# Where the first four attention states are made, and where the loads of chunks 4 to 9 stand in SyncE's queue

## The chip, the cores and the metric

One core of a Trainium2 chip runs the whole program: linear attention (RWKV style), then an MLP with squared ReLU, then an MLP with a soft-max gated activation and a layer norm. The metric is the device time of one execution in microseconds (us); lower is better. Instructions stand in a fixed order on each of TensorE (PE), VectorE (DVE), ScalarE (ACT), GpSimd (POOL) and SyncE (SP, which here issues every DMA); each of the five works through its own list in order and waits on semaphores for the others.

## What is computed

```python
# attention: B=4, H=8, S=768, D=48; one 48x48 state per batch and head
for t in range(S):
    kt, vt, rt = k[:, :, t], v[:, :, t], r[:, :, t]
    y[:, :, t] = einsum(rt, state + u*kt (x) vt)
    state = w * state + kt (x) vt
x = relu(y_as_tokens @ w_in)          # 3072 x 384 @ 384 x 2048
x = (x * x) @ w_out                   # @ 2048 x 384
h = x @ w2_in                         # @ 384 x 1024
solu = h * softmax(h)
out = (layernorm(solu) * g_ln) @ w2_out   # @ 1024 x 384
```

## The kernel before

The 3072 tokens are 24 chunks of 128 (chunk c is batch c % 4, piece c // 4 of the sequence). The attention of a chunk is a masked 128x128 score matrix per head plus the product with the state that the earlier pieces of its batch left. Chunks 0 to 3 are the first of their batch and need no state; for them a state must only be *made* for chunks 4 to 7. Chunks 4 and up run in half-chunks of 64 tokens.

The MLP works on blocks of 512 tokens (4 chunks). Its weights come as 64-bit floats: a weight *unit* (128x512 of `w_in`, 512 KB, or 128x384 of `w_out`, 384 KB) is loaded into one of six staging tiles `stg`, DVE turns it into 32-bit floats in three instructions (L610, L613, L616), ACT casts the high part (`wih` or `woh`, L628), POOL subtracts to get the low part (`wil` or `wol`, L629). `w1_conv` does that for one unit and then issues the load of the unit six places on, which must wait until POOL has freed the staging tile. There are 28 units: four groups of three `w_in` units and four `w_out` units.

The MLP's loop runs over *steps*: `p1` multiplies a block by 128 columns of `w_in` (nine matmuls on high and low parts: `wih,xh`, `wih,xl`, `wil,xh`), ACT and DVE make the squared ReLU and split it into `gh` and `gl`, `p2` multiplies by `w_out`. The first block has 20 steps: eight on 256 tokens, then twelve on 512. `p1` runs two steps ahead of `p2`.

What else has to happen in these 20 steps is hung on them by the table `side` (step to list of functions), in this order in the program: weight units (`w1_conv`); the states of chunks 0 to 3 (`first_state`, at steps 0 to 3: `prep_kt` scales k on DVE into `ktg`, L375; `pe_u` multiplies, L451; `dve_first` scales the product into the state `sg`, L491); and for chunks 4 to 7 the attention itself: `prep_rk` scales k and r (`kd`, L351, and the two halves of `mv`, L356, all on POOL), `prep_b` makes the diagonal (L385, L386 on POOL, L397 on DVE, L402 on POOL), `pe_u` (L464) and `pe_scores` (L437) run on PE, `dve_state` (L501, L502) and `dve_mask` (L481) on DVE, `pe_av_sub` (L541) on PE, and `split_x` hands the result to the MLP. `load_chunk` issues a chunk's loads: `kd` (224 KB, L241), `tok` (384 KB, L242), two `mv` (96 KB each, L244) and two `vs` (96 KB each, L246). Chunks 8 and up come in later steps (table `ev`).

The side table is not the final order. The framework's scheduler plays the program against its own estimate of times and writes each engine's list; what a function issues can stand well away from the step that it hangs on. A function's instructions keep their data dependences, and a few carry an explicit order (`add_manual_dep`, without a semaphore). So the lists of the built program are read beside the diff below.

Of the kernel before, what the change touches and what calls it, by code (L numbers as in the profile page):

```python
# [177 lines left out]
def rwkv_moe_moe2_kernel(ctx, tc, rkd, tok, tk2, wd, w, u, w_in, w_out, w2_in, w2_out, g_ln, out):  # L178
    nc = tc.nc
# [45 lines left out]
    def load_chunk(c, slots=None):  # L225
        if c >= NC:
            return
        i = (c % B) * CPB + c // B
        if c < B:
            if slots:  # L230
                rk_t[c] = wp.tile([GR, 2, NP, C], F32, tag=slots[0], name="rkw")
                tok_t[c] = wp.tile([C, 3, DM], F32, tag=slots[1], name="tokw")
            else:
                rk_t[c] = mv[c][:GR]
                tok_t[c] = ap.tile([C, 3, DM], F32, tag="tok", name="tok")
            nc.sync.dma_start(out=rk_t[c], in_=rkd[i])
            nc.sync.dma_start(out=tok_t[c], in_=tok[i])
            return
        rk_t[c] = ap.tile([GR, NP, C], F32, tag="kd", name="kd")
        tok_t[c] = ap.tile([128, 3, DM], F32, tag="tok", name="tok2")[:, :2]  # L240
        nc.sync.dma_start(out=rk_t[c], in_=rkd[i, :, 1])  # L241
        nc.sync.dma_start(out=tok_t[c], in_=tk2[i, :, :2])  # L242
        for j in range(2):
            nc.sync.dma_start(out=mv[c % 2][RO[j]:RO[j] + D, j], in_=rkd[i, RO[j]:RO[j] + D, 0])  # L244
            q = slice(CH * j, CH * (j + 1))
            nc.sync.dma_start(  # L246
                out=vs[c % 2][q, j].rearrange("q s p d -> q (s p d)"), in_=tk2[i, q, 2]
            )
# [117 lines left out]
    def prep_kt(c):  # L366
        if c < B:
            k, t = tok_t[c][:, 1], kpt
            i0, i1 = (a.rearrange("q (a j d) -> q a j d", a=NP, j=2) for a in (k, t))
            o = ktg[c % 2].rearrange("q (a j d) -> q a j d", a=NP, j=2)  # L370
        else:
            i0 = tok_t[c][:, 1].rearrange("q (s e) -> q s e", s=2)
            i1 = kp2.rearrange("q p d -> q (p d)").unsqueeze(1).to_broadcast([128, 2, NP * D])
            o = ktg[c % 2].rearrange("q (s e) -> q s e", s=2)
        nc.vector.tensor_tensor(out=o, in0=i0, in1=i1, op=ALU.mult)  # L375
# [33 lines left out]
    def pin(ins):  # L409

        tc.keep_in_program_order(ins)
# [33 lines left out]
    def pe_u(c, ub=1):  # L445
        kt = ktg[c % 2]
        if c < B:
            for p in range(NP):
                for j in range(2):
                    h = 2 * p + j  # L450
                    nc.tensor.matmul(  # L451
                        ps[RO[j]:RO[j] + D, ub, p * D:(p + 1) * D],
                        kt[:, h * D:(h + 1) * D],
                        tok_t[c][:, 2, h * D:(h + 1) * D],
                        start=(p == 0),
                        stop=(p == NP - 1),
                    )
            return
        for s in range(1 if c // B == CPB - 1 else 2):
            for p in range(NP):  # L460
                for j in range(2):
                    q = slice(CH * j, CH * (j + 1))
                    o = (s * NP + p) * D
                    pin(nc.tensor.matmul(  # L464
                        ps[RO[j]:RO[j] + D, ub, o:o + D], kt[q, o:o + D], vs[c % 2][q, j, s, p],
                        start=True, stop=True,
                    ))
# [19 lines left out]
    def dve_first(c, ub):  # L487

        for j in range(2):
            q = slice(RO[j], RO[j] + D)  # L490
            nc.vector.tensor_tensor(  # L491
                out=sg[c][q], in0=ps[q, ub, :NP * D].rearrange("p (a e) -> p a e", a=NP),
                in1=wm[q, 1].to_broadcast([D, NP, D]), op=ALU.mult,
            )
# [33 lines left out]
    def pe_av_sub(c, yb):  # L528

        rk_t.pop(c)  # L530
        tok_t.pop(c)
        y = ps[:, yb, :DM].rearrange("p (k i) -> p k i", k=KD)
        for s in range(2):
            i = slice(s * CH, (s + 1) * CH)
            for piece in (True, False):
                for k in range(KD):
                    p = KD if piece else k
                    for j in range(2):
                        v = vs[c % 2][:KR[j], j, s].rearrange("q p d -> q (p d)")
                        m, o = (64, p * D + 16 * k - D) if piece else (D, p * D)  # L540
                        pin(nc.tensor.matmul(  # L541
                            y[64 * j:64 * j + m, k, i], v[:, o:o + m], mv[c % 2][:KR[j], j, p, i],
                            start=True, stop=True,
                        ))
        xr_t[c] = y
# [47 lines left out]
    def load_unit(src, kind, g, eng):  # L593


        n = DM if kind else 512
        st = mp.tile([128, 512], src.dtype, tag="stg", bufs=NST, name="stg")[:, :n]
        if kind:
            eng.dma_start(out=st, in_=src[g * 128:(g + 1) * 128])
        else:  # L600
            eng.dma_start(out=st, in_=src[g[0] * 128:(g[0] + 1) * 128, g[1] * 512:(g[1] + 1) * 512])
        return st
# [32 lines left out]
        W1 += [(0, (k, g)) for k in range(KD)] + [(1, 4 * g + q) for q in range(4)]  # L635
    w_ld, w_st = [0], []

    def w1_load(n=1):
        for _ in range(n):
            if w_ld[0] < len(W1):  # L640
                kind, g = W1[w_ld[0]]
                w_st.append((kind, g, load_unit((w_in, w_out)[kind], kind, g, nc.sync)))
                w_ld[0] += 1

    def w1_conv():
        kind, g, st = w_st.pop(0)
        weight_tiles(kind, g // 4 if kind else g[1])
        if kind:
            split(st, woh[g // 4][:, g % 4], wol[g // 4][:, g % 4])()
        else:  # L650
            split(st, wih[g[1]][:, g[0]], wil[g[1]][:, g[0]])()
        w1_load()
# [239 lines left out]

    def first_state(c):
        prep_kt(c)
        pe_u(c, 0)
        dve_first(c, 0)
        del tok_t[c]


# [1 line left out]
    side = {i: [] for i in range(first_full)}  # L901
    first_m = {m: i for i, (n, m, c0, sz) in reversed(list(enumerate(steps))) if n == 0}
    for g in range(4):
        for q, n in enumerate((2, 2, 3) if g < 3 else (1, 1, 1, 1)):
            side[first_m[4 * g + q]] += [w1_conv] * n
    for c in range(4):
        side[c].append(lambda c=c: (first_state(c), load_chunk(4 + c) if c < 2 else None))
    for q, c in enumerate(range(4, 8)):
        t = 5 + 3 * q + (q > 0)
        side[t].append(lambda c=c: (prep_rk(c), put_state(c, 0), prep_kt(c), prep_b(c)))  # L910
        side[t + 1].append(lambda c=c: (pe_u(c), pe_scores(c), dve_state(c), dve_mask(c)))
        side[t + 2].append(lambda c=c: (pe_av_sub(c, 0), load_chunk(c + 2)))
        side[t + 3].append(lambda c=c: split_x(c))
    p1_at = [0]

# [18 lines left out]
    for q, t in enumerate(visits):  # L934
        c = 2 * B + q
# [11 lines left out]
    for i in range(first_full, nsteps):  # L947
        n, m, c0, sz = steps[i]
# [111 lines left out]
```

## Time and profile before

| | |
|---|---|
| median of 3 runs | 730.61 us (727.38 to 731.11) |
| the profiled execution | 729.26 us, span 727.6 us |
| PE busy in the span | 701.8 us (96%), 25.8 us without a matmul |
| DVE, ACT, POOL busy | 407.1 us (56%), 319.5 us (44%), 265.9 us (37%) |
| mean granted TensorE clock | 0.996 of full speed |
| chain that ended last | 85% of the span on PE, DMA, DVE, POOL 1% each |

The profiled execution lies 1.35 us below the median and inside the range of the three runs. Busy times are summed over the whole program; the shares of one stretch can be quite other, and the table of windows further down gives them by stage. A row of a timeline reads: start, duration, engine, line, operation, output<-input, shape, count, and in brackets the idle time before it with what ended it. A row with x2 is two instructions in one stretch. On SP the duration is that of issuing.

### The profile page before, as it was taken

How to read it: one execution, taken by the hardware profiler on the slowest of the kernel's cores; microseconds unless marked ns; L12 is line 12 of the kernel's file. 1: busy time of each engine (PE TensorE's matmuls, PEld its weight loads, DVE VectorE, ACT ScalarE, POOL GpSimd, SP SyncE). 2: the span in 40 equal slices, each digit the busy share in tenths (PEclk: the TensorE clock that was granted, in tenths of full speed). 3: DMA queues.
4: the chain of work that ended last, by engine and by line, in shares of the span. 5: the costliest groups of instructions: out<-in, count | busy, mean ns of one | idle time of the engine just before them, and what ended most of it. 6: DMA issues, size and time to landing. Idle time of an engine off the chain costs nothing.

```text
span 727.6 us, 13207 instructions
## 1 busy us (share of the span) xinstructions
PE 701.8 (96%) x5152; PEld 600.6 (83%) x5152; DVE 407.1 (56%) x752; ACT 319.5 (44%) x621; POOL 265.9 (37%) x297
## 2 busy tenths in 40 slices
PE   4789989999999999999999999999999999999996
PEld 3678868888888888888888888888899999999996
DVE  7899884444443334333322266515868777677771
ACT  1444645545455545544554455634333233322241
POOL 6969787254523333333221023802303030300000
PEclk9999999999999999999999999999999999999999
DMA  8956631222322212322160016221112000000001
GB/s 284 290 191 196 199 111 57 78 84 74 115 81 87 58 49 62 110 64 67 46 198 25 12 41 212 79 87 44 57 64 66 22 23 23 12 22 23 23 34 37
DMA packets 33832, 61.93 MB, mean 85 GB/s; under 512 B 7265, under 2 KB 16098, under 8 KB 33762
## 3 DMA queue, kind: packets, MB, share of 16 engines
q1 hardware_dynamic: 33762, 61.01, 26.7%
q8 instruction: 42, 0.69, 0.4%
q14 instruction: 28, 0.23, 0.1%
HBM read 48.41 MB, written 9.44 MB: 80 GB/s over the span
## 4 chain that ended last, share of the span: by engine, by line
PE 85%; DMA 1%; DVE 1%; POOL 1%; issue 1%; ACT 0%; SPq 0%; POOLq 0%; ACTq 0%
PE ps L670 8%; PE ps L692 8%; PE ps L689 8%; PE ps L688 8%; PE ps L672 8%; PE ps L671 8%; PE ps L838 5%; PE ps L837 5%; PE ps L840 5%; PE ps L774 5%; PE ps L776 5%; PE ps L775 5%; PE ps L821 3%; PE ps L514 2%; PE ps L437 2%; PE ps L464 2%
## 5 line engine op out<-in xcount | busy, mean ns | idle before, releaser
L678 DVE TENSOR_TENSOR gl<-ps,gh 128x512 fp32r<-128x512 f32 (+1 forms) x100 | 66.6, 667 | 178.7 <-ACT gh L677 177.4
L670 PE MATMUL ps<-xh,wih 128*128 128x512 f32 (+1 forms) x300 | 117.5, 393 | 1.7 <-DVE gl L678 1.1
L672 PE MATMUL ps<-xh,wil 128*128 128x512 f32 (+1 forms) x300 | 115.2, 385 | 2.3 <-POOL wil L629 2.3
L688 PE MATMUL ps<-gh,woh 128*128 128x512 f32 (+1 forms) x300 | 113.2, 383 | 1.9 <-ACT gh L677 1.9
L671 PE MATMUL ps<-xl,wih 128*128 128x512 f32 (+1 forms) x300 | 114.7, 383 | 0.1
L689 PE MATMUL ps<-gh,wol 128*128 128x512 f32 (+1 forms) x300 | 113.3, 384 | 0.0
L675 ACT ACTIVATE ps<-ps 128x512 f32<-128x512 f32 (+1 forms) x100 | 56.3, 564 | 129.3 <-PE ps L672 128.8
L356 POOL TENSOR_TENSOR mv<-mv,pt 48x512 f32<-48x512 f32 x40 | 51.4, 1286 | 87.5 <-DMA mv<-in_rkd_dram 87.0
L692 PE MATMUL ps<-gl,woh 128*128 128x512 f32 (+1 forms) x300 | 83.2, 382 | 0.0
L672 PEld LDWEIGHTS ps<-xh,wil 128*128 128x128 f32 x300 | 56.7, 189 | 14.4 <-POOL wil L629 3.4
L670 PEld LDWEIGHTS ps<-xh,wih 128*128 128x128 f32 x300 | 56.6, 189 | 13.9 <-DVE gl L678 1.5
L688 PEld LDWEIGHTS ps<-gh,woh 128*128 128x128 f32 x300 | 55.9, 188 | 13.0 <-ACT gh L677 2.1
L837 PE MATMUL ps<-w2oh,lth 128*128 128x384 f32 x192 | 65.2, 339 | 0.2 <-ACT lth L830 0.2
L671 PEld LDWEIGHTS ps<-xl,wih 128*128 128x128 f32 x300 | 56.8, 190 | 10.3 <-DVE xl L590 0.3
L838 PE MATMUL ps<-w2ol,lth 128*128 128x384 f32 x192 | 65.2, 340 | 0.0
L689 PEld LDWEIGHTS ps<-gh,wol 128*128 128x128 f32 x300 | 56.1, 189 | 11.0 <-issue 0.2
L692 PEld LDWEIGHTS ps<-gl,woh 128*128 128x128 f32 x300 | 55.7, 189 | 10.9
L677 ACT CAST gh<-ps 128x512 fp32r<-128x512 f32 (+1 forms) x100 | 56.9, 570 | 2.8
L676 ACT ACTIVATE ps<-ps 128x512 f32<-128x512 f32 (+1 forms) x100 | 56.4, 566 | 2.8
L774 PE MATMUL ps<-w2ih,xh 128*128 128x512 f32 x144 | 57.4, 399 | 0.0
L775 PE MATMUL ps<-w2il,xh 128*128 128x512 f32 x144 | 56.9, 395 | 0.0
L776 PE MATMUL ps<-w2ih,xl 128*128 128x512 f32 x144 | 56.8, 395 | 0.0
(122 smaller groups left out, 1174.9 us busy)
## 6 DMA issues: line engine op xcount, KB each, us to landing
stg<-in_w_in_dram SPq DMA_DIRECT2D x18, 512.0 KB, 6.2
stg<-in_w_out_dram SPq DMA_DIRECT2D x24, 384.0 KB, 4.1
tok<-in_tk_dram SPq DMA_DIRECT2D x20, 384.0 KB, 3.8
x2d<-stg SPq DMA_DIRECT2D x18, 256.0 KB, 2.5
x2r<-x2d SPq DMA_DIRECT2D x6, 768.0 KB, 4.9
out_dram<-ob SPq DMA_DIRECT2D x24, 192.0 KB, 1.9
kd<-in_rkd_dram SPq DMA_DIRECT2D x20, 224.0 KB, 3.9
mv<-in_rkd_dram SPq DMA_DIRECT2D x40, 96.0 KB, 2.4
```

What stands on the lines that cost most here:

```text
L670: nc.tensor.matmul(hp, wih[g][:, k, f], xh[:, k, cs], start=(k == 0), stop=False)
L671: nc.tensor.matmul(hp, wih[g][:, k, f], xl[:, k, cs], start=False, stop=False)
L672: nc.tensor.matmul(hp, wil[g][:, k, f], xh[:, k, cs], start=False, stop=(k == KD - 1))
L678: nc.vector.tensor_tensor(out=gl, in0=hp, in1=gh.bitcast(F32), op=ALU.subtract)
L688: nc.tensor.matmul(acc[e], woh[m // 4][:, m % 4, f], gh, start=start, stop=False)
L689: nc.tensor.matmul(acc[e], wol[m // 4][:, m % 4, f], gh, start=False, stop=False)
L692: nc.tensor.matmul(acc[e], woh[m // 4][:, m % 4, f], gl, start=False, stop=stop)
L774: nc.tensor.matmul(o, x2h[j][:, k, s], w2["ih"][:, k, fs], start=(k == 0), stop=False)
L775: nc.tensor.matmul(o, x2h[j][:, k, s], w2["il"][:, k, fs], start=False, stop=False)
L776: nc.tensor.matmul(o, x2l[j][:, k, s], w2["ih"][:, k, fs], start=False, stop=(k == KD - 1))
L837: nc.tensor.matmul(o, hi[:, m], w2["oh"][:, m], start=(m == 0), stop=False)
L838: nc.tensor.matmul(o, hi[:, m], w2["ol"][m // 4][:, m % 4], start=False, stop=False)
```

## The change

Three things change in the side table. The states of chunks 0 to 3 are made at steps 2, 5, 8 and 11 in place of 0, 1, 2 and 3, and their products go to PSUM bank 1, the one that later chunks use for theirs, in place of bank 0. The loads of chunks 4 to 9 hang on steps 2, 5, 8, 12, 14 and 17; before, chunks 4 and 5 were loaded right behind the states of chunks 0 and 1, and chunks 6 to 9 behind `pe_av_sub` of chunks 4 to 7. Each of these loads gets an order: on SP it may not stand ahead of the last weight load that the program had issued by then. And `pe_av_sub` is put ahead of the other functions of its step.

```diff
+    w_last = [None]
+    def behind_weights(load, *args):
+        n = len(nc.cur_bb.bb.instructions)
+        load(*args)
+        for i in nc.cur_bb.bb.instructions[n:]:
+            if i.engine == nc.sync.engine:
+                tc.add_manual_dep(
+                    i, w_last[0].name,
+                    mybir.DependencyInfo(mybir.DependencyClass.NoSync, mybir.DependencyReason.DATA),
+                    reason="behind_weights",
+                )
...
                 w_ld[0] += 1
+                w_last[0] = nc.cur_bb.bb.instructions[-1]
...
     def first_state(c):
         prep_kt(c)
-        pe_u(c, 0)
-        dve_first(c, 0)
+        pe_u(c)
+        dve_first(c, 1)
         del tok_t[c]
...
-    for c in range(4):
-        side[c].append(lambda c=c: (first_state(c), load_chunk(4 + c) if c < 2 else None))
+    for c, t in enumerate((2, 5, 8, 11)):
+        side[t].append(lambda c=c: first_state(c))
+    for c, t in zip(range(4, 10), (2, 5, 8, 12, 14, 17)):
+        side[t].append(lambda c=c: behind_weights(load_chunk, c))
...
-        side[t + 2].append(lambda c=c: (pe_av_sub(c, 0), load_chunk(c + 2)))
+        side[t + 2].insert(0, lambda c=c: pe_av_sub(c, 0))
```

The built lists differ from the first loads of chunk 4 to PE's 415th row of some 2610, that is inside the first block and the start of the second; behind that they are the same on every engine. Three places follow. Lines of the changed program are 15 to 17 higher from L640 on.

SP's list, first before: the loads of chunks 4 and 5 (all but `tok`) stand ahead of the seventh weight unit, `stg_189`, and its successors.

```order
L267 DMA ub2_85<-in_u_dram 64x4x48 x2
L241 DMA kd_361<-in_rkd_dram 112x512
L244 DMA mv0_95<-in_rkd_dram 48x512
L246 DMA vs0_97<-in_tk2_dram 64x384
...
L241 DMA kd_448<-in_rkd_dram 112x512
L246 DMA vs1_98<-in_tk2_dram 64x384
L244 DMA mv1_96<-in_rkd_dram 48x512
L599 DMA stg_189<-in_w_out_dram 128x384
```

SP's list now. `stg_189` to `stg_449` follow `ub2` directly; `stg_463` is the sixteenth weight unit, whose staging tile POOL frees with the low part of unit `stg_341`.

```order
L599 DMA stg_449<-in_w_out_dram 128x384
L601 DMA stg_456<-in_w_in_dram 128x512
L601 DMA stg_463<-in_w_in_dram 128x512
L241 DMA kd_476<-in_rkd_dram 112x512
L242 DMA tok2_477<-in_tk2_dram 128x768
L244 DMA mv0_95<-in_rkd_dram 48x512
L246 DMA vs0_97<-in_tk2_dram 64x384
L244 DMA mv0_95<-in_rkd_dram 48x512
L246 DMA vs0_97<-in_tk2_dram 64x384
L241 DMA kd_567<-in_rkd_dram 112x512
L242 DMA tok2_568<-in_tk2_dram 128x768
```

All six loads of chunk 4 moved from ahead of ten weight units to behind them. The next weight unit comes only after those of chunk 5.

POOL's list, before: the scaling of chunks 4 and 5 stands among and ahead of the low parts of units `stg_189` to `stg_341`.

```order
L351 TENSOR_TENSOR kd_361<-kd_361,pt_80 112x512
L629 TENSOR_TENSOR wol_335<-stg_133,woh_334 128x384
L356 TENSOR_TENSOR mv0_95<-mv0_95,pt_80 48x512 x2
L351 TENSOR_TENSOR kd_448<-kd_448,pt_80 112x512
L356 TENSOR_TENSOR mv1_96<-mv1_96,pt_80 48x512 x2
L629 TENSOR_TENSOR wol_335<-stg_189,woh_334 128x384
L629 TENSOR_TENSOR wil_481<-stg_212,wih_480 128x512
L629 TENSOR_TENSOR wil_481<-stg_243,wih_480 128x512
L629 TENSOR_TENSOR wil_481<-stg_341,wih_480 128x512
```

POOL's list now, the same place and on to the end of chunk 4's scaling.

```order
L629 TENSOR_TENSOR wol_335<-stg_133,woh_334 128x384
L629 TENSOR_TENSOR wol_335<-stg_189,woh_334 128x384
L629 TENSOR_TENSOR wil_443<-stg_212,wih_442 128x512
L629 TENSOR_TENSOR wil_443<-stg_243,wih_442 128x512
L629 TENSOR_TENSOR wil_443<-stg_341,wih_442 128x512
L629 TENSOR_TENSOR wol_724<-stg_348,woh_723 128x384
L351 TENSOR_TENSOR kd_476<-kd_476,pt_80 112x512
L385 TENSOR_TENSOR tok2_477<-tok2_477,ub2_85 128x384
L629 TENSOR_TENSOR wol_724<-stg_409,woh_723 128x384
L356 TENSOR_TENSOR mv0_95<-mv0_95,pt_80 48x512 x2
```

Six instructions (one `kd` and two `mv` for each of chunks 4 and 5) went behind four weight units and more.

PE's list, before: chunk 4's scores (L437) stand behind a whole `p1` and a `p2`.

```order
L464 MATMUL ps_63<-vs0_97,ktg0_89 48x48 x16
L670 MATMUL ps_63<-xh_203,wih_480 128x512
...
L692 MATMUL ps_63<-gl_619,woh_334 128x256 x3
...
L689 MATMUL ps_63<-gh_682,wol_754 128x512
L437 MATMUL ps_63<-mv0_95,kd_361 64x64 x16
```

PE's list now: the first scores stand after two matmuls of that `p1`.

```order
L707 MATMUL ps_63<-gl_542,woh_334 128x256 x3
L464 MATMUL ps_63<-vs0_97,ktg0_89 48x48 x16
L685 MATMUL ps_63<-xh_203,wih_442 128x512
L686 MATMUL ps_63<-xl_204,wih_442 128x512
L437 MATMUL ps_63<-mv0_95,kd_476 64x64
L687 MATMUL ps_63<-xh_203,wil_443 128x512
```

One row of scores (x1) moved forward past a `p2` and most of a `p1`; the other fifteen stand behind the `p2` that follows.

## Rows read from the trace of the kernel before

**Rows 1.** Windows: busy time (instructions) of each engine by stretch, clock, DMA share, GB/s.

```profile
24.00:33.00 9.00, 6.05 (x35) 5.59 (x34) 6.35 (x14) 4.04 (x12) 9.00 (x9) 0.81 0.87 218
...
45.00:60.00 15.00, 13.89 (x174) 12.57 (x174) 14.68 (x31) 9.33 (x23) 9.68 (x10) 1.00 0.68 223
60.00:88.00 28.00, 27.97 (x294) 22.77 (x291) 26.93 (x53) 16.26 (x33) 23.94 (x24) 1.00 0.65 196
88.00:105.00 17.00, 14.78 (x160) 11.42 (x159) 12.99 (x23) 6.44 (x12) 13.26 (x13) 1.00 0.50 153
105.00:165.00 60.00, 60.00 (x582) 49.72 (x581) 29.02 (x56) 31.50 (x64) 31.46 (x31) 1.00 0.23 70
```

**Rows 2.** Timeline of PE, 28 to 104 us: rows that stood idle first.

```profile
28.70 0.76 PE L688 MATMUL ps<-gh,woh 128*128 128x256 f32 x3 [1.88 <-ACT gh L677]
...
49.80 0.39 PE L670 MATMUL ps<-xh,wih 128*128 128x256 f32 x1 [1.11 <-DVE gl L678]
...
97.95 0.51 PE L672 MATMUL ps<-xh,wil 128*128 128x512 f32 x1 [0.18 <-POOL wil L629]
...
100.61 1.59 PE L541 MATMUL ps<-mv,vs 112*64 112x64 f32 x48 [0.99 <-DVE mv L481]
...
103.92 0.50 PE L672 MATMUL ps<-xh,wil 128*128 128x512 f32 x1 [1.06 <-POOL wil L629]
```

**Rows 3.** Timeline of DVE, 44 to 93 us.

```profile
44.98 2.62 DVE L375 TENSOR_TENSOR ktg<-tok,kpt 128x384 f32<-128x384 f32 x2
...
49.32 0.42 DVE L678 TENSOR_TENSOR gl<-ps,gh 128x256 fp32r<-128x256 f32 x1
...
92.76 0.55 DVE L397 TENSOR_REDUCE b<-tok 128x8 f32<-128x384 f32 x1 [3.82 <-POOL mv L402]
```

**Rows 4.** Timeline of POOL, 33 to 90 us.

```profile
33.17 1.29 POOL L351 TENSOR_TENSOR kd<-kd,pt 112x512 f32<-112x512 f32 x1
...
39.47 2.60 POOL L356 TENSOR_TENSOR mv<-mv,pt 48x512 f32<-48x512 f32 x2
...
45.82 1.35 POOL L629 TENSOR_TENSOR wil<-stg,wih 128x512 fp32r<-128x512 f32 x1 [0.24 <-ACT wih L628]
...
54.51 1.02 POOL L386 TENSOR_TENSOR tok<-tok 128x384 f32<-128x384 f32 x1
...
58.75 1.37 POOL L402 TENSOR_SCALAR_AFFINE_SELECT mv<-b 64x512 f32<-64x512 f32 x2
...
79.75 2.64 POOL L356 TENSOR_TENSOR mv<-mv,pt 48x512 f32<-48x512 f32 x2 [2.52 <-DMA mv<-in_rkd_dram]
...
89.14 1.28 POOL L351 TENSOR_TENSOR kd<-kd,pt 112x512 f32<-112x512 f32 x1 [1.73 <-DMA kd<-in_rkd_dram]
```

**Rows 5.** Source view of L375: duration in ns min/median/max of twenty.

```profile
L375 DVE TENSOR_TENSOR ktg<-tok,kp x20: 542/671/2347, 56.1 to 361.5; 128x384 f32<-128x384 f32 x20
```

**Rows 6.** Timeline of SP, 48 to 84 us.

```profile
48.25 0.38 SPq L601 DMA_DIRECT2D stg<-in_w_in_dram  x1
...
74.92 0.42 SPq L244 DMA_DIRECT2D mv<-in_rkd_dram  x1
...
83.83 0.39 SPq L241 DMA_DIRECT2D kd<-in_rkd_dram  x1
```

**Rows 7.** The page's DMA issues: count, KB each, median us from issue to landing.

```profile
kd<-in_rkd_dram SPq DMA_DIRECT2D x20, 224.0 KB, 3.9
```

**Rows 8.** Timeline of PE, 54 to 61 us.

```profile
54.27 0.56 PE L451 MATMUL ps<-tokw,ktg 128*48 128x48 f32 x16
...
55.58 0.40 PE L670 MATMUL ps<-xh,wih 128*128 128x512 f32 x1
...
57.65 0.52 PE L692 MATMUL ps<-gl,woh 128*128 128x256 f32 x3
...
59.30 0.92 PE L464 MATMUL ps<-vs,ktg 64*48 64x48 f32 x32
60.16 0.50 PE L670 MATMUL ps<-xh,wih 128*128 128x512 f32 x1
```

## The prediction

> **What bounds the kernel now.** I read the windows by stage first, since the page's 96% for PE is an average. From 105 us on PE is busy without a break for 60 us [rows 1], and it stays so up to the last part of the program, which the change does not touch. PE's idle time that the change can reach lies where its lists differ: between some 45 and 105 us. There PE is busy 13.89 of 15, 27.97 of 28 and 14.78 of 17 us [rows 1], so 1.11 + 0.03 + 2.22 = 3.36 us are open. That is the ceiling of the gain from removed waits: 0.46% of the time.
>
> PE's own timeline says who ends these waits [rows 2]. At 49.80 PE waits 1.11 us for DVE's `gl`. At 97.95, 100.61 and 103.92 it waits 0.18, 0.99 and 1.06 us, twice for a low part that POOL makes (`wil`), once for DVE's mask of chunk 6.
>
> Why these are late is read on DVE and POOL. DVE's `gl` of 49.32 stands behind two `ktg` that took 2.62 us together [rows 3], where one takes 0.54 at its shortest [rows 5]; POOL ran a `wil` at 45.82 just then [rows 4]. The late group has its cause earlier: DVE stands still for 3.82 us before 92.76 [rows 3]: the sums of chunk 9's diagonal need a buffer that POOL frees with chunk 7's diagonal. POOL had itself waited 1.73 us for chunk 7's `kd` at 89.14, and 2.52 us for an `mv` of chunk 6 at 79.75 [rows 4]. All weight units of DVE's list queue behind that stop. DVE is busy 26.93 of 28 us from 60 to 88 [rows 1], so it cannot win such a stop back soon.
>
> **The change, part by part.** No work is added or removed: the matmuls, DVE, ACT and POOL instructions and loads are the same, in another order. So the sum consists of waits only.
>
> *First wait (49.80).* POOL no longer does chunk 4's and 5's scaling from 33.17 to 42.07: two `kd` of 1.29 and two pairs of `mv` of 2.60, 7.8 us [rows 4]. The low part of the second unit behind them is then done about 1.3 us sooner, before the two `ktg` start; undisturbed they take 2 x 0.54 = 1.1 us in place of 2.62. DVE's list also puts `gl` one instruction (0.6 us) earlier. Against that, six 256-column matmuls (three span 0.52 with their drain [rows 8], 0.12 apart; 0.7 us for six) now stand ahead of chunk 3's attention on PE, which delays DVE's start here. `gl` then ends near 49.74 - 1.5 - 0.6 + 0.7 = 48.3, and PE asked for it at 49.80 - 1.11 = 48.69. I take 1.0 of the 1.11 us as gained (0 if the two `ktg` are held up as before).
>
> *A new wait, at chunk 4's scores.* These loads now stand behind the sixteenth weight unit, which needs the staging tile that POOL's `wil` of 45.82 frees at 47.17 [rows 4], 47.9 with the 0.7 us above. Its load was issued at 48.25 before [rows 6], so no earlier than 47.9 now, and `kd` 0.4 us behind it, at 48.3. It lands 3.9 us later by the median [rows 7], or 5.3 us later by the nearest row: the `kd` issued at 83.83, 0.4 us behind a 512 KB weight load, was there at 89.14 [rows 4, 6]. That is 52.2 or 53.6. Then POOL needs, in its new list, `kd` (1.29), `tok` (1.0), one `wol` (1.0) and the pair of `mv` (2.6), 5.9 us [rows 4]: 58.1 to 59.5. The `mv` load itself is hidden: issued near 49.4, there 4.8 us later as from 74.92 to 79.75 [rows 4, 6]. PE comes to the first scores as follows [rows 8]: its first 512-column `p1` started at 55.58; less 1.0 gained, less 0.5 for the product of chunk 2 (54.27) that moved behind, 54.1; plus 2.07 for the `p1`, 0.4 for the `p2` rest, 0.86 for L464 and 0.57 for two matmuls: 58.0. So PE waits 0.1 to 1.5 us; I take 1.2, near the row that is like it. The outer bounds are 0 and 2.5 (DVE's `ktg` falls in with POOL's rows here, and each can hold up the other).
>
> *The late group (97.95 to 103.92).* DVE's list up to the last `w_in` unit has less in it than before: chunk 6's mask, its state, two diagonals and a `ktg` moved behind, some 4 us, and the stop of 3.82 us has no cause there: chunk 9's diagonal, which made it, is one of the two that moved behind. POOL then sets the pace: from `kd` of chunk 4 to that unit it has 16 instructions of 1.3, 16 of 1.0 and four pairs of 1.4 us [rows 4], 42.7 us, without a gap from 53.6: done at 96.3. PE came to that place at 103.92 - 1.06 = 102.86; less the earlier waits gained, 2.2, less 2.6 for chunk 6's product (1.5) and five matmuls of 0.23 that now stand behind, plus the new 1.2: 99.3. That leaves 3.0 us of room. The third group's last `wil` is tighter. POOL's list up to it holds 23.5 us: done at 77.1. PE has, from the scores at 59.2, 60 matmuls of 0.23, nine of 0.12 and four groups of small ones (0.5, 0.9, 1.5 [rows 2, 8], and one of about 1.0, as many matmuls as the 0.9) ahead of it, 18.8 us: 78.0. The room there is 0.9 us. I take 2.23 us as gained, less 0.5 for smaller waits (POOL rows that run long, the scores' bank 1 shared with the states): 1.7.
>
> *Bank, loads of chunks 6 to 9, order of `pe_av_sub`.* The first states in bank 1 must each wait for DVE's reading of the one before; in the new list a whole `p1` or `p2` (2 us) lies between, which covers it; without that cover one wait costs under 1 us. SP stops behind these loads until a `tok` tile is read; the weight units behind it are needed 5 us or more later.
>
> Sum: - 1.0 + 1.2 - 1.7 = - 1.5 us. The profiled execution, 729.26 us, would become 727.8. It lies 1.35 us under the median of the three runs, and I set the forecast against that median: 730.61 - 1.5 = 729.1 us.
>
> **The rivals.** *The scores don't wait.* If `kd` lands in 3.9 us or less, and POOL's rows keep their lengths, the 1.2 and the 0.5 fall away: - 3.2, 727.4 us. For it: the median [rows 7]. Against it: the like row with 5.3.
>
> *POOL and DVE hold each other up: slower.* In the new lists POOL has no gap from 54 to 97 us, and six `ktg` of DVE fall into that time. The two at 44.98 cost 2.62 - 1.08 = 1.5 us more beside POOL's `wil` [rows 3, 4], 0.77 each; four of them stand ahead of the third group's last low part, which comes 3.1 - 0.9 = 2.2 us too late. With 1.5 at the scores that makes 3.7 us lost against 1.0 + 2.2 gained: + 0.5. If these waits let the granted clock fall as after 28.70 (0.81 over 9 us, so in part the lower level of 1.2 GHz, after 2.95 us without matmuls [rows 1, 2]), up to 1.7 us more go: + 2.2, 732.8 us. It decides from the point where POOL loses more than the 0.9 us of room before the third group. Against it: the median `ktg` is 0.67 us, at a POOL that was busy 23.94 of 28 us [rows 1, 5]. The Trainium skill bears on this rival ("SBUF — State Buffer", section "Who interferes with whom"): a VectorE instruction with two inputs in SBUF and a GpSimd instruction that reads SBUF share a port, and the later one waits for the whole of the other. The row of 2.62 agrees; by the rule every one of the six could pay, by the median few do.
>
> *An even trade.* The new wait reaches 2.5 us and part of the late group stays: about 730.6 us.
>
> **How the numbers follow.** Forecast 0.45, no wait at the scores 0.25, even trade 0.17, slower 0.13. A measurement of this kernel tells about 0.5% (3.65 us) from no change, as three runs spread over 3.7 us. The ceiling of 3.36 us lies under that bound, so a gain over 0.5% needs the second case and some luck in the runs: 0.11. A loss over 0.5% needs the slower case with waits beyond its price: 0.07. Within: 0.82. The range runs from 726.8 (the second case, and half a microsecond of spread) to 732.4 (the even trade with its spread, and most of the slower case); what is beyond is about 0.2.
>
> **What would show it.** In the changed profile PE's timeline has no wait for `gl` near 49, the two `ktg` near 46 take about 1.1 us together, and no 3.8 us stop of DVE ends near 93. A wait for POOL's `mv` (L356) stands before the first L437 near 58, and the waits for `wil` near 100 are under 0.5 us in all. The forecast is wrong if the wait at the scores is over 2.5 us, if the third group's `wil` makes PE wait over 1 us, if the clock falls behind one of these, or if PE's idle time between 45 and 105 us is not between 0.5 and 3.5 us.

## The result, and the profile of the changed kernel

| kernel | median (range), us | ratio to the kernel before |
|---|---|---|
| before, 11 runs beside | 729.71 (727.38 to 733.59) | |
| changed, 11 runs | 734.8 (730.94 to 736.47) | 1.0055 [1.0039, 1.0072] |

The change makes the kernel about 0.55% slower; 729.1 us was forecast, with 732.4 as the upper end. The eleven times fall in two groups that go with the mean granted clock: four of 730.9 to 731.9 us at 0.994 to 0.996, seven of 733.5 to 736.5 us at 0.988 to 0.992. The profiled execution is the fastest of them (730.94 us, span 729.1, clock 0.996), so this section shows only what the faster group loses. (These are medians of eleven runs on one chip; the forecast was set against the 730.61 us of three.) PE is busy 703.1 us (96%) there, DVE 406.6 (56%), ACT 320.0 (44%), POOL 267.9 (37%). In the changed file all lines from L670 on have numbers higher by 15 to 17.

Windows, as in [rows 1]:

```profile
24.00:33.00 9.00, 6.03 (x37) 5.51 (x36) 7.81 (x16) 4.38 (x12) 9.00 (x9) 0.85 0.81 239
33.00:45.00 12.00, 10.98 (x103) 9.44 (x102) 9.31 (x18) 3.77 (x8) 4.96 (x5) 0.97 0.45 129
45.00:60.00 15.00, 14.55 (x147) 12.76 (x148) 12.09 (x26) 9.42 (x23) 8.50 (x8) 1.00 0.84 225
60.00:88.00 28.00, 26.43 (x268) 21.66 (x267) 27.51 (x52) 14.93 (x30) 27.24 (x26) 1.00 0.62 193
88.00:105.00 17.00, 16.02 (x166) 12.83 (x165) 15.05 (x30) 9.05 (x19) 14.77 (x14) 1.00 0.53 162
105.00:165.00 60.00, 60.00 (x619) 49.04 (x618) 29.54 (x56) 29.43 (x60) 36.84 (x36) 1.00 0.26 79
```

PE idles 0.45 + 1.57 + 0.98 = 3.00 us between 45 and 105, against 3.36 before: the waits were not removed, they moved. From 105 us on it is busy as before. PE's timeline, as in [rows 2]:

```profile
28.80 0.62 PE L703 MATMUL ps<-gh,woh 128*128 128x256 f32 x3 [1.87 <-ACT gh L692]
...
58.68 0.33 PE L437 MATMUL ps<-mv,kd 48*64 48x64 f32 x2 [0.44 <-POOL mv L356]
...
64.53 0.50 PE L685 MATMUL ps<-xh,wih 128*128 128x512 f32 x1 [1.57 <-DVE gl L693]
...
101.11 0.50 PE L687 MATMUL ps<-xh,wil 128*128 128x512 f32 x1 [0.98 <-POOL wil L629]
```

The wait of 49.80 is gone. The one at the first scores is 0.44 us. New is 1.57 us at 64.53 behind DVE's `gl`, and at 101.11, the last `w_in` unit's low part, 0.98 us is left. DVE, as in [rows 3]:

```profile
45.93 1.02 DVE L375 TENSOR_TENSOR ktg<-tok,kpt 128x384 f32<-128x384 f32 x2
...
48.08 0.42 DVE L693 TENSOR_TENSOR gl<-ps,gh 128x256 fp32r<-128x256 f32 x1
...
54.85 0.56 DVE L375 TENSOR_TENSOR ktg<-tok,kp 128x384 f32<-128x384 f32 x1 [1.01 <-DMA tok<-in_tk_dram]
...
58.82 2.60 DVE L375 TENSOR_TENSOR ktg<-tok,kp 128x384 f32<-128x384 f32 x1 [1.55 <-DMA tok<-in_tk_dram]
...
63.79 0.68 DVE L693 TENSOR_TENSOR gl<-ps,gh 128x512 fp32r<-128x512 f32 x1
```

The two `ktg` of 45.93 take 1.02 us together and `gl` comes at 48.08. But at 58.82 DVE stands 1.55 us for chunk 5's `tok`, and the `ktg` that follows takes 2.60 us. POOL, as in [rows 4]:

```profile
53.33 1.29 POOL L351 TENSOR_TENSOR kd<-kd,pt 112x512 f32<-112x512 f32 x1 [1.43 <-DMA kd<-in_rkd_dram]
...
57.36 2.62 POOL L356 TENSOR_TENSOR mv<-mv,pt 48x512 f32<-48x512 f32 x2
...
98.50 1.31 POOL L385 TENSOR_TENSOR tok<-tok,ub 128x384 f32<-128x384 f32 x1 [0.95 <-DMA tok<-in_tk_dram]
...
99.77 1.29 POOL L629 TENSOR_TENSOR wil<-stg,wih 128x512 fp32r<-128x512 f32 x1
```

While that `ktg` takes 2.60 us (to 61.42), POOL runs the second half of the `mv` pair and, from 59.94 to 60.95, a product of L386. At 98.50 POOL waits 0.95 us for chunk 8's `tok`, with the last `wil` behind it. SP, as in [rows 6], and the page's DMA issues, as in [rows 7]:

```profile
48.53 0.42 SPq L241 DMA_DIRECT2D kd<-in_rkd_dram  x1
...
49.05 0.38 SPq L242 DMA_DIRECT2D tok<-in_tk_dram  x1
...
52.60 0.35 SPq L242 DMA_DIRECT2D tok<-in_tk_dram  x1
...
87.82 6.76 SPq L599 DMA_DIRECT2D stg<-in_w_out_dram  x3
...
94.63 0.90 SPq L242 DMA_DIRECT2D tok<-in_tk_dram  x2
```

```profile
kd<-in_rkd_dram SPq DMA_DIRECT2D x20, 224.0 KB, 3.6
tok<-in_tk_dram SPq DMA_DIRECT2D x20, 384.0 KB, 4.2
```

Chunk 5's `tok` is the eighth of twelve loads that SP issues from 48.53 to 56.6; it was there 6.2 us after its issue. Chunk 8's went out only at 94.63, behind three weight loads that kept SP for 6.76 us.

At the first product of L514 (143.73 us before, 144.49 now) the profiled execution is 0.76 us behind, and so at the last row of matmuls (719.62, 720.39). The other 0.7 us of the span lie behind it. There SP, at the end of its list and with no load left, stands still for 1.56 us between two instructions (726.27 to 727.83); the kernel before has no such stop. In the traces of this case all eight profiles of kernels with all six loads tied have one of 1.3 to 1.6 us, the eight others have none; from the end of the last matmul to the end of the span the first take 7.0 to 7.8 us, the others 5.7 to 6.6. So part of what the order costs (some 1.2 us by these profiles) has nothing to do with waits for a load. What SP waits for there, no view shows, and no run tests it.

### The profile page after: what moved, and what is told of

The parts are those of the page before. It is cut to its first block, busy times and chain, and to the rows that moved or that the text cites. A ratio compares the mean times of both kernels' runs of the same rounds, so it can differ in the third digit from the quotient of the medians.

```text
span 729.1 us, 13204 instructions
## 1 busy us (share of the span) xinstructions
PE 703.1 (96%) x5152; PEld 600.9 (82%) x5152; DVE 406.6 (56%) x752; ACT 320.0 (44%) x621; POOL 267.9 (37%) x297
## 4 chain that ended last, share of the span: by engine, by line
PE 85%; POOL 6%; DMA 4%; issue 3%; DVE 1%; SPq 0%; ACT 0%; POOLq 0%; ACTq 0%
PE ps L685 8%; PE ps L707 8%; PE ps L703 8%; PE ps L704 8%; PE ps L687 8%; PE ps L686 8%; PE ps L853 5%; PE ps L852 5%; PE ps L855 5%; PE ps L789 5%; PE ps L791 5%; PE ps L790 5%; PE ps L836 3%; PE ps L514 2%; PE ps L437 2%
```

## The experiments

Each ratio is to the kernel before run beside it on the same chip (medians 729.2 to 730.3 us), so ratios can be compared between chips and medians only within one: e1 to e4 ran on one chip, f1 to f4 on another, g1 to g4 on a third, h1 and h2 on a fourth. In e4 and h1 an edit higher up in the file shifts the lines by another 6 or 7.

| run | median (range), us; runs | ratio to before |
|---|---|---|
| e1 changed kernel again | 732.67 (731.22 to 734.19); 6 | 1.0047 [1.0031, 1.0063] |
| e2 loads not tied | 727.68 (726.85 to 729.61); 12 | 0.9974 [0.9964, 0.9984] |
| e3 states early, loads tied | 731.59 (730.63 to 733.56); 11 | 1.0031 [1.0020, 1.0041] |
| e4 chunk 5's keys behind `gl` | 731.71 (730.86 to 733.99); 11 | 1.0033 [1.0021, 1.0046] |
| f2 chunks 4, 5 tied | 733.91 (733.12 to 735.70); 4 | 1.0069 [1.0049, 1.0090] |
| f3 chunks 6 to 9 tied | 727.07 (725.59 to 729.10); 5 | 0.9961 [0.9946, 0.9976] |
| g1 all but 5 tied | 736.39 (732.84 to 740.35); 9 | 1.0093 [1.0068, 1.0117] |
| g2 all but 4 tied | 731.41 (730.10 to 733.37); 10 | 1.0018 [1.0002, 1.0034] |
| h1 split ahead of chunk 8 | 731.08 (729.78 to 732.97); 12 | 1.0031 [1.0020, 1.0042] |
| f4, h2 pauses put into before | 742.64 (741.47 to 745.76); 4 and 748.69 (746.54 to 749.72); 4 | 1.0185 [1.0153, 1.0218], 1.0270 [1.0252, 1.0287] |
| f1, g3, g4 changed, one execution each | 731.16, 731.75, 737.86 | |

### First: which part costs (e1 to e4)

The changed kernel again, without an edit:

> The changed kernel itself. Its eleven executions fell in two groups, four near 731.4 us (granted clock 0.994 to 0.996) and seven near 734.9 (0.988 to 0.992). Theory A: the slower group is the faster one plus a fall of TensorE's clock right behind PE's wait of 1.57 us at 64.5 us, which DVE makes because the scaled keys (L375) of chunk 5 wait for their load. Then more than half of the executions lie 3 to 5 us above the others again, and a profile that catches one shows the granted clock below 1.00 between 64 and 72 us and nowhere else than in the kernel before. Rival B: the clock falls behind the wait of 0.98 us for a low part at 101 us, so between 101 and 110 us. Rival C: it falls at the first steps, before 45 us, where the loads changed too.

It gave 732.67 us, and a profile like the first: stops of 0.42, 1.58 and 1.08 us, clock 0.996. Its six times run from 731.22 to 734.19 without a gap between two groups, and the profiled one is the fastest, so it decides between none of the theories.

The loads at their new steps, but with no order behind the weights:

```diff
-        side[t].append(lambda c=c: behind_weights(load_chunk, c))
+        side[t].append(lambda c=c: load_chunk(c))
```

> The change without the order that ties the loads of chunks 4 to 9 behind the weights; the states stay at steps 2, 5, 8, 11 in bank 1. In the built list the loads of kd, mv and vs of chunks 4 and 5 stand ahead of the weights again, and chunk 5's tok one weight unit behind chunk 4's. Theory A: chunk 5's keys don't wait 1.5 us, PE's wait at 64.5 goes, and the time is within 0.2% of before or up to 0.3% faster, in one group. Rival B (POOL's packed list and the late group are the cause): POOL's list has the scaling early again, so B expects no loss either, but with the wait at 64.5 still there. If it is as slow as the change (0.5%), the moved states are the cause and not the loads.

727.68 us, faster than the kernel before over the whole interval. So the rest of the change is worth 0.26%, and the order behind the weights costs 732.67 - 727.68 = 5.0 us on the same chip. Of the 3.2 us between the two profiled executions (728.1 and 731.22 us, spans 726.2 and 729.4), 1.85 are there at the first L514 (142.98 and 144.83) and the rest behind the last matmul, where e2 does not have SP's stop (1.34 us in e1).

The states back to the early steps, loads tied:

```diff
-    for c, t in enumerate((2, 5, 8, 11)):
+    for c, t in enumerate((0, 1, 2, 3)):
```

> The change with the states of chunks 0 to 3 made at steps 0 to 3 as before (in bank 1), the loads tied behind the weights as in the change. Theory A: chunk 1's product, which frees the tile that chunk 5's tok is loaded into, comes some steps earlier only if the list shows it; the load still stands behind the sixteenth weight unit, so the keys of chunk 5 wait 0 to 1.5 us: time between 0 and 0.5% above before. Rival (the moved states cause the loss): no loss against before.

731.59 us; the stop of 64.5 is gone, and 2.28 us (for DVE's mask, 86.36) and 1.53 us (`wil`, 104.63) stand in its place. So the moved states are not the main cause (e1, on the same chip, is 1.1 us above). Theory C, the clock at the first steps, is not settled by it: in this profile the clock is at half for 6.8 us from 27.4, twice as long as in the first.

Chunk 5's `ktg` put behind a `gl` in DVE's list, one `add_manual_dep`:

```diff
+        if c == B + 1:
+            tc.add_manual_dep(
+                nc.cur_bb.bb.instructions[-1], gl_ins[first_m[4]].name,
...
```

> The change with one instruction of DVE moved: the scaled keys of chunk 5 (L375) stand behind the gl of the first 512-column step in DVE's list and not seven instructions ahead of it. Loads and states as in the change. Theory A: DVE's stop for chunk 5's load no longer delays gl, PE's wait of 1.57 us goes to under 0.5, the clock stays at 1.00 there, all executions fall in one group, and the median drops by 3.5 to 6 us against the change: 728 to 731 us. Rivals B and C: the median stays near 734 and two groups remain.

The stop of 64.5 is gone here too, but the time is only about 1 us less than e1's, not the 3.5 to 6 that theory A had. The profiled execution is the slowest of the eleven (733.99 us, clock 0.990). PE's timeline, and the windows behind it:

```profile
87.14 1.59 PE L547 MATMUL ps<-mv,vs 112*64 112x64 f32 x48 [1.75 <-DVE mv L487]
...
92.27 0.73 PE L691 MATMUL ps<-xh,wih 128*128 128x512 f32 x1 [1.95 <-DVE gl L699]
```

```profile
91.00:92.00 1.00, 0.00 (x0) 0.00 (x0) 1.00 (x3) 0.00 (x0) 1.00 (x2) 1.00 0.84 263
92.00:93.00 1.00, 0.73 (x2) 0.64 (x3) 1.00 (x3) 0.00 (x0) 1.00 (x1) 0.68 1.04 352
93.00:94.00 1.00, 1.00 (x3) 0.79 (x3) 0.87 (x2) 0.00 (x0) 1.00 (x2) 0.50 0.81 189
94.00:95.00 1.00, 1.00 (x4) 0.73 (x3) 0.90 (x2) 0.00 (x0) 1.00 (x2) 0.50 0.08 23
95.00:96.00 1.00, 1.00 (x4) 0.79 (x3) 0.95 (x2) 0.00 (x0) 0.92 (x2) 0.61 0.00 0
```

The stops came again 25 us later, and behind the second the granted clock goes to 0.50, the level of 1.2 GHz, for 3.4 us. So theory A, a single late load, is not enough: take one stop away and the next thing late stops PE.

### Second: whose loads (f2, f3, g1, g2)

```diff
-        side[t].append(lambda c=c: behind_weights(load_chunk, c))
+        side[t].append(lambda c=c: behind_weights(load_chunk, c) if c < 6 else load_chunk(c))
```

> The changed kernel with only the loads of chunks 4 and 5 tied behind the weights; chunks 6 to 9 are issued free. Theory A (it is chunk 5's late keys that cost): the stop at 64.5 us stays at 1.3 to 1.8 us and the ratio to the kernel before is 1.003 to 1.006, as with all six tied. Theory E (the ties of the later chunks cost, by the waits in 85 to 105 us): the ratio is 0.997 to 0.999, as with none tied, though the stop at 64.5 us is there.

f3 has the same condition the other way round.

> The other half: chunks 4 and 5 free, chunks 6 to 9 tied. Theory A: no wait over 1 us in 55 to 75 us, ratio 0.997 to 0.999. Theory E: waits of 1 us and more in 85 to 105 us, ratio 1.002 to 1.006.

f2 is 733.91, f3 727.07 us. So the order of chunks 4 and 5 is what costs, as theory A had it, and that of chunks 6 to 9 costs nothing (f3's ratio is 0.9961, e2's without any order 0.9974); theory E falls. Neither has SP's stop at the end, so the 6.8 us between the two lie elsewhere. But the stop at 64.21 (1.59 us) is not all of it. f2 has 1.23 us at 100.61, and 1.51 and 0.69 at 111.61 and 113.45, with the clock at half for 3.4 us behind these. f3 also beats both kernels, e2 does too. In f3 SP issues the small loads of chunks 4 and 5 long before the weights' rush and only the `tok` later, for which DVE does not wait there; a `kd` and the `tok` of chunk 5:

```profile
27.70 0.31 SPq L241 DMA_DIRECT2D kd<-in_rkd_dram  x1
...
54.48 0.33 SPq L242 DMA_DIRECT2D tok<-in_tk_dram  x1
```

The kernel before did so as well (a `kd` at 24.83). With these loads tied, none goes out between 24 and 48 us.

g1 and g2 free one of the two chunks (`load_chunk(c) if c == 5 else ...`, and 4):

> The changed kernel with chunk 5's loads free and those of chunk 4 and of chunks 6 to 9 tied. With both free the ratio was 0.9961, with both tied 1.0055. Theory A5 (chunk 5 alone costs: its keys, 6 us behind its issue, stop VectorE): ratio 0.995 to 0.999 and no wait over 1 us in 55 to 75 us. Theory A4 (each tie pushes some 1.2 MB of loads from 24 to 30 us, where the queue has room, into the rush behind 48 us, and chunk 4's is enough for it): ratio 1.001 to 1.006, with waits for POOL's or VectorE's work on chunk 4 in 55 to 70 us.

> The other half: chunk 4's loads free, chunk 5's and those of 6 to 9 tied. Theory A5: VectorE still waits for chunk 5's keys and TensorE 1 to 1.8 us behind it at 62 to 67 us; ratio 1.003 to 1.006. Theory A4: the rush is half as long, chunk 5's keys come 2 us earlier, and the ratio is 0.996 to 1.001.

(A chunk's loads are 224 + 384 + 4 x 96 KB, 1.0 MB, not 1.2.) Theory A5 falls: without chunk 5's order the kernel is the slowest but for those with pauses put in, 1.0093, and in g2, where chunk 5's order stays, PE has no stop over 0.3 us between 55 and 80. Theory A4 has the sign of both, but g1 is worse and g2 slightly worse than its ranges. In g1 PE stops 4.21 us near 100 for a diagonal of POOL's, with the clock at half for 6.8 us; in g2 2.87 us near 95 for DVE's `xl`, half for 3.4 us. The ties do not add up: the stop comes out at another place each time. That each tie shifts the scheduler's lists is the likely reason; it was not followed through the lists.

### Third: where the slower half of the executions loses (f1, g3, g4)

> The changed kernel once more, for the profile of an execution with the lower mean clock: seven of its first eleven timed runs had a mean granted clock of 0.988 to 0.992 and took 733.5 to 736.5 us, the other four 0.994 to 0.996 and 730.9 to 731.9 us, and both profiles so far were of the latter. Theory A (the clock falls behind the stop for chunk 5's keys): an execution of 733 us or more shows a granted clock of 0.85 to 0.95 in 60 to 88 us or in 88 to 105 us, behind waits of TensorE of 1.5 us and more. Theory D (the clock falls only in the fill before 45 us, by chance): it shows a full clock behind 45 us and less than 0.75 in 24 to 33 us. An execution of 731 us tells nothing new of this.

731.16 us, with no stop at 64.5 and one of 2.50 us at 101.46, and a full clock behind it (PE's row, then a window):

```profile
101.46 0.50 PE L687 MATMUL ps<-xh,wil 128*128 128x512 f32 x1 [2.50 <-POOL wil L629]
...
101.50:108.00 6.50, 6.50 (x38) 5.14 (x40) 6.36 (x12) 2.98 (x6) 6.35 (x6) 1.00 0.20 61
```

(What the expectations call the third weight group is the one with index 3, the last of the four.)

> The changed kernel once more, for the profile of one of its executions with a mean granted clock of 0.988 to 0.992 (nine of its eighteen so far; all three profiles were of the others). In the profiles so far each fall of the clock is some 3.4 us at half of full speed, 1.7 us lost: one of them in every kernel at 28 to 33 us, a second behind stops that follow each other closely. If that is the cause of the slower half, an execution of 733 us or more shows two falls more than one of 731 us, each behind stops of TensorE in 40 to 115 us; if the cause is another, it shows one fall, at 28 to 33 us, and the time is lost elsewhere.

731.75 us, stops of 0.51, 1.57 and 1.22 us; one fall of the clock, 27.7 to 34.5 us, 6.8 us long.

> The same once more, with the same expectation: 733 us or more with two further falls of the granted clock behind stops in 40 to 115 us, or 731 us with one fall alone, at 28 to 33 us.

737.86 us, clock 0.990. PE's rows and windows:

```profile
61.49 0.32 PE L437 MATMUL ps<-mv,kd 48*64 48x64 f32 x2 [0.54 <-POOL mv L356]
...
104.58 0.80 PE L687 MATMUL ps<-xh,wil 128*128 128x512 f32 x1 [2.55 <-POOL wil L629]
```

```profile
101.00:102.00 1.00, 0.97 (x12) 0.42 (x8) 0.14 (x1) 0.73 (x2) 0.02 (x1) 1.00 0.88 327
102.00:103.00 1.00, 0.03 (x1) 0.00 (x0) 1.00 (x3) 0.00 (x0) 1.00 (x1) 1.00 1.05 324
103.00:104.00 1.00, 0.00 (x0) 0.00 (x0) 1.00 (x4) 0.81 (x3) 1.00 (x2) 0.90 1.08 224
104.00:105.00 1.00, 0.42 (x1) 0.42 (x2) 1.00 (x3) 1.00 (x3) 0.97 (x2) 0.50 0.62 150
105.00:106.00 1.00, 1.00 (x3) 0.74 (x3) 0.97 (x3) 0.39 (x1) 1.00 (x2) 0.50 0.09 35
109.00:110.00 1.00, 1.00 (x4) 0.79 (x3) 0.93 (x3) 0.03 (x1) 1.00 (x2) 0.50 0.41 163
110.00:111.00 1.00, 1.00 (x5) 0.80 (x4) 1.00 (x3) 0.00 (x0) 1.00 (x2) 0.69 0.00 0
```

With one stop of 2.55 us the clock goes to half, from 103.8 to 110.6. From the end of that stop to the first L514 PE needs 46.2 us (104.58 to 150.78) where it needs 43.4 in the first profile (101.11 to 144.49), so 2.8 us are lost. Besides, this execution was 2.9 us later than the first already at 45 us, 1.4 of them because POOL's `wil` of the first group kept PE waiting 2.54 us at 29.38, where it is 1.10. These are 5.7 of the 6.3 us by which its first L514 is late. So in the one slower execution that was caught, itself slower than any of the eighteen of the first run, e1 and f1, less than half of the loss is the clock behind the stop at the last split, as much lies ahead of 45 us, and nothing is a fall behind 64.5. That the others of the slower half lose in the same places is not shown by it.

Why is there 1.57 + 0.98 in three of five profiles and 2.5 in two? DVE and POOL in g4:

```profile
61.40 0.56 DVE L375 TENSOR_TENSOR ktg<-tok,kp 128x384 f32<-128x384 f32 x1 [1.33 <-DMA tok<-in_tk_dram]
```

```profile
60.16 2.95 POOL L356 TENSOR_TENSOR mv<-mv,pt 48x512 f32<-48x512 f32 x2
```

Here it is POOL's pair of `mv` that is long (2.95) and the `ktg` is short (0.56); in the first profile it is 2.62 and 2.60. The other three profiles go with this: e1 and g3 have the long `ktg` (2.66, 2.71) and the stop at 64.5, f1 the long `mv` (2.90), a `ktg` of 0.56 and none. With no stop at 64.5 PE comes to the last split 1.5 us earlier, and waits there for the same thing. The Trainium skill ("SBUF — State Buffer", "Who interferes with whom") says that a VectorE instruction with two inputs in SBUF contends with a GpSimd one that reads SBUF, and that the order of issue decides who is blocked. The pairs of rows agree.

### Fourth: is it the last split (h1)

One instruction moved on POOL: chunk 8's first product behind the last `wil`.

```diff
+            wil_ins[g] = nc.cur_bb.bb.instructions[-1]
...
+        if c == 2 * B:
+            tc.add_manual_dep(
+                nc.cur_bb.bb.instructions[-1], wil_ins[2, 3].name,
...
```

> The changed kernel with one instruction moved on POOL: chunk 8's first product, which waits 0.95 us for its tokens at 98.5 us, stands behind the last split of the third weight group and not ahead of it. So the split is done some 2.2 us earlier. Theory B (the slower half of the executions is a fall of the clock behind TensorE's stop for this split): the stop at 101 us, 0.98 us in the faster executions and 2.5 us in the slower ones, is under 0.4 us, no execution has a mean clock under 0.992, and the median is 728.8 to 730.5 us, ratio 0.999 to 1.001. Rival R (the stops only move on): one or more stops that add up to over 1.5 us in 95 to 125 us, executions with a clock of 0.988 to 0.991 still there, ratio 1.003 to 1.006.

```profile
64.32 0.50 PE L692 MATMUL ps<-xh,wih 128*128 128x512 f32 x1 [1.58 <-DVE gl L700]
...
100.18 0.50 PE L694 MATMUL ps<-xh,wil 128*128 128x512 f32 x1 [0.26 <-POOL wil L635]
...
103.57 0.50 PE L710 MATMUL ps<-gh,woh 128*128 128x512 f32 x1 [0.82 <-ACT gh L699]
```

The split is done 0.9 us earlier (100.13 for 101.06), not 2.2. The stop there is 0.26 us, and of twelve executions one has a clock of 0.992 and none less, where of the first eighteen of the changed kernel eleven (not nine, as said above) had 0.988 to 0.992 and eight of them 0.990 or less; the slowest is 732.97 us. That is theory B's sign for the slower half, with the reservation that the changed kernel was not run beside h1 on this chip. The ratio is the rival's: 1.0031, where theory B had 0.999 to 1.001. Of the 1.9 us above the kernel before, 0.82 can be a new stop for `gh` right behind the split, the 1.58 us at 64.32 are untouched, and 1.49 are SP's stop at the end of the program, with which neither theory reckoned. The rival's other signs, stops over 1.5 us in 95 to 125 us (0.26 + 0.82 here) and clocks of 0.988 to 0.991, are not there.

### Fifth: what a stop does to the clock (f4, h2)

In the kernel before, 165 to 400 us have no stop of PE at all. There VectorE's subtraction is repeated at a few steps, with the same values:

```diff
+        for _ in range(1 + {38: 7, 46: 8, 54: 8, 62: 9, 70: 10, 78: 8, 80: 8}.get(i, 0)):
-        nc.vector.tensor_tensor(out=gl, in0=hp, in1=gh.bitcast(F32), op=ALU.subtract)
+            nc.vector.tensor_tensor(out=gl, in0=hp, in1=gh.bitcast(F32), op=ALU.subtract)
```

> The kernel before, with VectorE's subtraction of gl done 8 to 11 times instead of once at steps 38, 46, 54, 62, 70, 78 and 80 of the first feed-forward (same values, 0.69 us for each further one), some 38 us apart, so that TensorE has to stop in a stretch where it otherwise never does (165 to 400 us, granted clock 1.00). Some 3.4 to 6 us of each pause are covered by the two steps that TensorE works ahead, so I expect one stop of 0.5 to 4 us at each. Theory C1 (one stop of 1.5 us is enough for the clock to fall): behind every stop over 1.5 us the granted clock of the next 4 us is 0.5, and the time is the sum of the stops and some 1.7 us for each of them above the kernel before. Theory C2 (a single stop of up to 2 us costs only itself, and stops close together are needed): the clock stays at 1.00 behind single stops up to 2 us and falls at the pair of steps 78 and 80 at most; the time is the sum of the stops above the kernel before.

The single stops came out as 0.36 to 1.20 us, too short for theory C1's test, and the clock stayed at 1.00; the pair made one of 5.27 us, with half the clock for 3.4 us behind it. So h2, with {38: 12, 46: 13, 54: 12, 62: 12, 70: 12}:

> The kernel before with VectorE's subtraction of gl done 13 or 14 times at steps 38, 46, 54, 62 and 70 (same values). Where it was done 8 to 11 times the stops were 0.36 to 1.2 us and the clock stayed at 1.00; I expect five stops of 1.8 to 3.2 us here, some 40 us apart. Theory C1 (one stop of that length is enough): the granted clock is at half behind each of the five, for 3.4 us or for twice that. Theory C3 (it depends on how the stop falls, as the two profiles with one stop of 2.5 us at the third group showed, one with a fall and one without): behind some of the five it falls, behind others not. Theory C2 (single stops cost only themselves): it falls behind none, and the time is the sum of the five stops, 9 to 16 us, above the kernel before.

Each pause became two stops some 4 us apart: 0.83 and 1.86, 0.36 and 2.60, 0.59 and 1.86, 0.62 and 1.89, 0.76 and 1.86 us. The rows of the first two:

```profile
225.12 0.50 PE L670 MATMUL ps<-xh,wih 128*128 128x512 f32 x1 [1.86 <-DVE gl L678]
...
269.00 0.50 PE L670 MATMUL ps<-xh,wih 128*128 128x512 f32 x1 [2.60 <-DVE gl L678]
```

```profile
227.00:228.00 1.00, 1.00 (x4) 0.76 (x3) 0.00 (x0) 0.00 (x0) 0.00 (x0) 0.50 0.00 0
270.00:271.00 1.00, 1.00 (x6) 0.79 (x5) 0.00 (x0) 0.00 (x0) 0.00 (x0) 1.00 0.00 0
```

Behind the first and the third the clock was at half for 3.4 us, 1.7 us lost each; behind the other three, one of them with the longest stop of all, it was not. That is theory C3: stops of this length let the clock fall in some cases and not in others. With f1 and g4, one kernel with a stop of 2.5 us at the same place, the clock fell in one execution and not in the other.

## Why the prediction was wrong, step by step

*First wait.* Right: 1.11 us gone, the `ktg` 1.02 us (1.1 forecast), `gl` done at 48.50 (48.3).

*Wait at chunk 4's scores.* Right in kind, mis-sized: 0.42 to 0.76 us where 1.2 was taken, inside its 0.1 to 1.5. POOL's `kd` began at 53.33 (52.2 or 53.6 forecast).

*A wait that no step had.* The step on the loads followed chunk 4's `kd` and `mv` only. Chunk 5's `tok`, the eighth in the same queue, was not followed: DVE's list needs it at 57.3, it lands at 58.8, and with POOL's pair beside it `gl` is 1.57 us late for PE.

*The late group.* This is the step that failed: 2.23 us of waits were taken as gained, less 0.5. POOL was to run "without a gap from 53.6" and have the last `w_in` unit done at 96.3, with 3.0 us of room. It was done at 101.06, 4.8 us later. From 53.33 to there POOL is busy 44.38 us, 1.7 more than the 42.7 of the sum (its terms add up to 42.4), and idle 3.35: for ACT's `wih` 0.68, for `vs` 0.37, twice for a `tok` that stood behind the weights, 0.38 and 0.95, and the rest in breaks under 0.2. So 1.7 us of the 4.8 are tied loads, the last of them right ahead of the last split; the other part is POOL's rows running longer than their row of before, ACT's `wih` and breaks. The prediction followed SP's stop behind the tied loads and called it harmless to the weights; it did not follow SP's stops at the weights (6.76 us at 87.82), which hold up the loads tied behind them, and POOL's list has those ahead of the splits. Gained: 2.23 - 0.98 = 1.25 us in the first profile. With the 2.50 and 2.55 of f1 and g4 it is a loss of 0.3, and the stop at 64.5 is not there.

*The sum.* - 1.11 + 0.44 - 1.25 + 1.57 = - 0.35 us of waits, against - 1.5. Yet the profiled execution is 0.76 us later at 144 us, though both profiles lose 1.7 us to the clock before 45: some 1.1 us are longer running of PE itself, whose lists before 144 us hold more breaks between small and large groups of matmuls (a group of L437 is now cut in two and thirty). That no work is added was right for the count of instructions, not for the time; which breaks cost it was not tried. With the 0.7 us behind the last matmul, to which the sum gave nothing, the faster executions lose 1.5 us of span. The median, 734.8, is another 3.9 us above the profiled execution; g4 alone shows where such time can go (the clock, and the steps before 45 us), and how it is shared in the rest stays open. That the order of chunks 4 and 5 brings the loss about is shown by f2 and f3; for it the sum had no term but the wait at the scores.

*The rivals.* "POOL and DVE hold each other up" is the one that came, with its point of decision: POOL losing its room ahead of a group's last low part, the last group instead of the third. Its price for the clock was too low, 1.7 us where the fall caught behind this stop cost 2.8. It was held to be one case with a chance of 0.13, where all five profiles of the changed kernel have the stop (0.98 to 2.55 us) and only one of them the fall. The sign "waits for `wil` near 100 under 0.5 us in all" failed too, with 0.98. The sign of "the clock falls behind one of these" was named as what would prove the forecast wrong, and in g4 it did. PE's idle time, 3.00 us, stayed inside the 0.5 to 3.5 that was said to show it right; idle time alone did not show the loss.

## What to carry to other kernels

An order that keeps a queue free for one kind of load is paid by those who wait for the other kind: look up every load that moves, to its last, and who stands behind it in the list of the engine that reads it. Where a stall is removed, follow the chain that set its end (here POOL's splits behind a late `tok`), since PE otherwise arrives earlier and waits there for the same thing. And a few microseconds of stops that add up to no more than before can still cost more, because the clock can come down behind them, in some executions and not in others. Last, look also at the end of the program: a part of this loss sits where nothing was changed.

## What was not expected of the hardware

The fall of the granted clock behind a stop is no fixed price. Behind 40 us it lasted 3.4 us at half (e2, e4, f2, f3, f4, g2, h2) or 6.8 us (g1, g4); a stop of 2.5 us had 6.8 us in g4 and none in f1, and of five nearly equal pauses in one execution two had it. Nor does it take stops of that length. In e2 and f3, the two fastest kernels, it falls behind two stops of 0.8 to 1.1 us some 2 us apart; f4 has stops of 0.98 and 0.83 us there, 6 us apart, and no fall. PE's rows and a window of e2:

```profile
40.33 1.16 PE L424 MATMUL ps<-rkw 48*128 48x128 f32 x8 [0.97 <-DVE xl L590]
42.31 0.91 PE L559 MATMUL ps<-atw,tokw 128*64 128x128 f32 x6 [0.82 <-DVE atw L473]
...
43.00:44.00 1.00, 1.00 (x13) 0.99 (x12) 0.97 (x2) 0.52 (x1) 1.00 (x2) 0.50 0.00 0
```

In every kernel of this case it falls once more at 27 to 36 us, behind two stops of 1.1 to 2.5 us, for 3.4 us or, in e3, e4 and g3, for 6.8. Up to the last matmul the first profile of the changed kernel (clock 0.996) is at half for 3.4 us in all, those of e4 and g4 (0.990) for 10.2; half of that is lost as far as PE has work in it. Behind the last matmul the clock falls in every profile, which costs PE nothing and still enters the mean: f1, with 0.994, has the same 3.4 us ahead of it as the first profile with 0.996.
